# First batch of a fused attention and gated MLP: both heads' scores on half the rows each, and a shift of the weights' narrowing moved to GpSimd

## The chip, the cores and the metric

The kernel runs on one core of a Trainium2 chip. The metric is the device time of one execution in microseconds (us). PE is TensorE, DVE VectorE, ACT ScalarE, POOL GpSimd, SP SyncE, which here issues nearly all DMAs.

## The reference, cut

```python
# q, k, v: (4, 8, 768, 64) float32; w_in, conv_w, w_out: float64
scores = q @ k.T / sqrt(64)                      # keep: key < 4, or 0 <= row - key < 128
a = softmax(where(keep, scores, -1e9))
x = (a @ v) as (4, 768, 512)
h = relu(x @ w_in)                               # d_ff 1024
conv = sum(conv_w[k] * h shifted by k - 1 rows)  # 3 taps
out = (h * sigmoid(conv)) @ w_out
```

## The kernel before, in words

The function `banded` does the work. It takes the heads in pairs, 4 pairs to a batch, and the rows in tiles of 128, 6 to a pair; one tile of one pair is a step. The first batch has 24 steps (first rows 0 to 383 of all pairs, then the others), and it is computed in plain float32, while later batches use split operands.

A step goes through `scores` (a product for each of the two heads into a PSUM tile `sc` of its own, two buffers; a masked minimum over each on DVE, L577; an exponential each on ACT, L580; sums and reciprocals on DVE, L583 and L584; a normalisation each on POOL, L586), `transp` (transposes of the weights, L603, copied out by ACT, L605) and `pv` (products with the values, L655 and L678).

Before a half of a pair comes to its scores, `prep32` transposes three tiles of the queries of both heads at once (head 0 on partitions 0 to 63, head 1 on 64 to 127), and ACT copies them out twice (L288 through `evac`): plane `j` is multiplied by column `j` of `headscale`, which is zero on the other head's partitions. So the score product of one head reads all 128 partitions of queries and keys (L378), half of them zeros.

During the same 24 steps the float64 weights are loaded and narrowed, 17 pieces, one a step from step 2 on: 16 of 128x512, and the three taps as 24x128. `narrow` computes on the two 32-bit words of a value: ACT multiplies the high words, read as floats, by 2^-112 into `low` (L118); DVE shifts that left by 3 into `w` (L121); DVE ors in the low words shifted right by 29 (L122); DVE ors in the sign bit of `low` (L123). `split` then rounds `w` on POOL (L130) and takes the remainder on DVE (L131). `w` and `low` take buffers from a set of three.

From step 12 on the MLP's products of the first 256 rows (L204 up, L239 down, the gate between them L211 to L227) are interleaved with the steps; in the later batches they fill TensorE. A planner puts each engine's instructions in one order ahead of time from its own costs; at run time every engine goes through its own in that order. `follow` adds a wait of one instruction on another.

Of the kernel before, what the change touches and what calls it, by code (L numbers as in the profile page):

```python
# [10 lines left out]
F32 = mybir.dt.float32  # L11
F32R = mybir.dt.float32r
I32 = mybir.dt.int32
AF = mybir.ActivationFunctionType
ALU = mybir.AluOpType
PSUM = bass.MemoryType.PSUM

P = 128
D = 64
# [5 lines left out]
SW = 2 * P + NS  # L25
# [13 lines left out]
def f(ap):  # L39
    return ap.bitcast(F32)  # L40
# [6 lines left out]
def follow(c, ins, other, reason):  # L47
    c.tc.add_manual_dep(ins.ins, other.ins.name, mybir.DependencyInfo(mybir.DependencyClass.Sync, mybir.DependencyReason.DATA),
                        reason=reason)
# [17 lines left out]
class Moe:  # L67
# [41 lines left out]
    def narrow(self, raw, to=None):  # L109


        if raw.dtype == F32:
            return raw
        nc, (rows, n) = self.c.nc, raw.shape[0:2]
        w = self.temp("st", 512, 3)[0:rows, 0:n] if to is None else to
        low = self.temp("st", 512, 3)[0:rows, 0:n]
        lo, hi, wi, li = raw[:, :, 0], raw[:, :, 1], w.bitcast(I32), low.bitcast(I32)
        first = nc.scalar.mul(low, f(hi), 2.0 ** -112)  # L118
        if len(getattr(self.c, "exps", [])) > 1:
            follow(self.c, first, self.c.exps[-2], "late")  # L120
        nc.vector.tensor_scalar(wi, li, 3, None, ALU.logical_shift_left)  # L121
        nc.vector.scalar_tensor_tensor(out=wi, in0=lo, scalar=29, in1=wi, op0=ALU.logical_shift_right, op1=ALU.bitwise_or)  # L122
        nc.vector.scalar_tensor_tensor(out=wi, in0=li, scalar=-0x80000000, in1=wi, op0=ALU.bitwise_and, op1=ALU.bitwise_or)  # L123
        return w

    def split(self, raw, parts, at):
# [147 lines left out]
class Attn:  # L274
# [74 lines left out]
    def prep32(self, g, half, s, kk, tag, ahead):  # L349

        c, nc, T, HTL, kw = self.c, self.nc, self.T, self.HTL, self.kw
        tiles = slice(HTL * half, HTL * half + HTL)

        def turn(nm):
            pt = self.mps.tile([P, HTL, P], F32, tag=tag, name=f"tr{nm}{g}{half}", bufs=3 if tag == "h" else 2)
            for t in range(HTL):
                c.pin(nc.tensor.transpose(pt[:, t, :], s.raw[nm, half][:, t].rearrange("p a d -> p (a d)"), c.ident))
            if nm == "q":
                s.X[half] = f(self.ap.tile([P, 2, HTL, P], F32R, tag="X", name=f"X{g}{half}", bufs=3))
                for j in range(2):  # L360
                    self.evac(s.X[half][:, j], pt, c.headscale[:, j:j + 1])
            else:
                s.kk = kk
                self.evac(kk[:, tiles, 0:P], pt, 1.0)
                if half == 0:
                    nc.scalar.copy(kk[:, :, P:kw], kk[:, 0:1, 0:kw - P].to_broadcast([P, T, kw - P]))
            ahead()

        s.plain = True
        return [lambda nm=nm: turn(nm) for nm in "qk"]  # L370

    def scores(self, s, t, pcs, lo, hi):

        half, u = divmod(t, self.HTL)
        X, kk = s.X[half], s.kk.rearrange("p a t k -> p a (t k)") if not s.plain else s.kk.rearrange("p t k -> p (t k)")
        if s.plain:
            for j, pc in enumerate(pcs):
                self.c.pin(self.nc.tensor.matmul(pc, X[:, j, u, :], kk[:, lo:hi], start=True, stop=True))  # L378
            return
        for j, pc in enumerate(pcs):  # L380
            self.c.pin(self.nc.tensor.matmul(pc, X[:, j, u, :], kk[:, j, lo:hi], start=True, stop=False))  # L381
            self.c.pin(self.nc.tensor.matmul(pc, X[:, j, u, :], kk[:, 2 + j, lo:hi], start=False, stop=True))  # L382
# [68 lines left out]
def banded(c):  # L451

    nc = c.nc
# [48 lines left out]
        nc.gpsimd.memset(sm, 1e-9)  # L502
    A.tiles = 0
    c.exps = []
    c.zero = nc.gpsimd.to_reg(0.0)
    c.part = cp.tile([P, 2], F32, name="part")
    nc.gpsimd.memset(c.part, 1.0)
# [43 lines left out]
    def scores(g, t):  # L551
        s = st[g]
        apart = g < NPAIR
        at = P if apart else 0
        lo = 0 if t == 0 else (t - 1) * KW
        mk = m0 if t == 0 else ((w1, w2) if apart else (m1, m2))[t > 1]
        cols = slice(at + NS if t == 0 else 0, at + KW)
        sm = sms[A.tiles % len(sms)]
        A.tiles += 1
        hf, u = divmod(t, 3)  # L560
        if u == 0:
            if apart:
                s.pe[hf] = m.room[g % 2][:, 0:6 * SW].rearrange("p (t h k) -> p t h k", t=3, h=2)
            else:
                s.pe[hf] = ap.tile([P, 3, 2, KW], F32, tag="pe", name=f"pe{g}_{hf}")
            if t == 0:
                nc.gpsimd.memset(s.pe[hf][:, 0, :, at:at + NS], 0.0)
        pe = s.pe[hf][:, u]
        pcs = [ps.tile([P, SW], F32, tag="sc", name=f"sc{g}_{t}_{j}", bufs=2) for j in range(2)]
        if t == 0:  # L570
            A.scores(s, t, [pc[:, KW:SW] for pc in pcs], lo, lo + P)
        else:
            A.scores(s, t, pcs, lo, lo + SW)
        for j, pc in enumerate(pcs):
            if t and not apart:
                nc.vector.copy_predicated(pc[:, KW:SW], before.bitcast(I32), pc[:, 0:P])
            nc.vector.tensor_tensor_reduce(out=pe[:, j, cols], in0=pc[:, P - at:SW][:, cols], in1=mk, op0=ALU.add, op1=ALU.min,  # L577
                                           scale=1.0, scalar=3.0e38, accum_out=sm[:, j:j + 1])
        for j in range(2):
            exp = nc.scalar.activation(pe[:, j, cols], pe[:, j, cols], AF.Exp, bias=sm[:, j:j + 1], scale=-1.0,  # L580
                                       accum_out=sm[:, 2 + 2 * j:3 + 2 * j])
        c.exps.append(exp)
        nc.vector.tensor_reduce(out=sm[:, 6:8], in_=sm[:, 2:6].rearrange("p (j e) -> p j e", e=2), op=ALU.add, axis=mybir.AxisListType.X)  # L583
        nc.vector.reciprocal(sm[:, 8:10], sm[:, 6:8])  # L584
        for j in range(2):
            nc.gpsimd.tensor_scalar(pe[:, j, cols], pe[:, j, cols], sm[:, 8 + j:9 + j], 1.0, ALU.mult, ALU.mult)  # L586
# [147 lines left out]
    for i in range(NST + DL):  # L734
        if i < NST:
            n, g, t = steps[i]
            if t % 3 == 0:
                for n1, at, *ends in coming(n):
                    new = prep(n1)
                    if at is None:  # L740
                        at = [ends[0] + (ends[1] - ends[0]) * (k + 1) / len(new) for k in range(len(new))]
# [16 lines left out]
        for slot in range(SLOTS):  # L758
            if slot == 0 and i < NST:
                first(i, scores, g, t)  # L760
            if slot == 0 and 0 <= i - D2 < NST:
                first(i, transp_sinks, *steps[i - D2][1:])
            if slot == (1 if i - D1 < NSTB else 2) and 0 <= i - D1 < NST:
                first(i, transp, *steps[i - D1][1:])
            for d, at in ((D2, 2), (DL, 1)):
                if slot == at and 0 <= i - d < NST and (i - d < NSTB) == (d == D2):
                    first(i, pv, *steps[i - d][1:])
                    if i - d + 1 in cuts:
                        while fill:
                            fill.pop(0)()  # L770
                        lo, hi, span = cuts[i - d + 1]
                        fill = m.pieces(lo, hi)
                        rate = len(fill) / (span - 0.5)
                        acc = 0.0
            acc += rate / SLOTS
            while acc >= 1.0 and fill:
                fill.pop(0)()
                acc -= 1.0
            while todo and i + (slot + 1) / SLOTS >= todo[0][0]:
                first(i, todo.pop(0)[1])  # L780
# [75 lines left out]
def attention_gated_mlp(ctx: ExitStack, tc: tile.TileContext, q, k, v, n_sink, window, w_in, conv_w, w_out, out):  # L856
    nc = tc.nc
    c = Ctx()
# [4 lines left out]
    con = ctx.enter_context(tc.tile_pool(name="con", bufs=1))  # L863
# [13 lines left out]
    nc.scalar.activation(fl[:, 0:1], fl[:, 1:2], AF.Exp)  # L877
    c.ident = con.tile([P, P], F32, name="ident")
    make_identity(nc, c.ident)
    c.headscale = con.tile([P, 2], F32, name="headscale")  # L880
    nc.gpsimd.memset(c.headscale, 0.0)
    for j in range(2):
        nc.gpsimd.memset(c.headscale[D * j:D * j + D, j:j + 1], -1.0 / math.sqrt(D))
    c.identr = con.tile([P, P], F32R, name="identr")
    nc.vector.tensor_copy(c.identr, c.ident)

# [19 lines left out]
    with tc.If(fast == 1) as cmp:  # L906
        with ExitStack() as es:
            c.es = es
            banded(c)
# [32 lines left out]
```

## Time and profile before

| | us |
|---|---|
| median of 3 runs | 474.14 (473.42 to 474.23) |
| the profiled execution, whole | 473.48 |
| its span, first to last instruction | 471.8 |
| mean granted TensorE clock | 0.997 of full speed |

Times in rows are from the span's start. The whole time has 1.7 us around the span. A row's busy time is what the profile shows for an instruction, blocked time within it included; two instructions of one engine can overlap a little in it.

### The profile page before, as it was taken

Reading aid. Unit: us, or ns where it says so; the run is one execution under the profiler, and the core shown is the slowest. Engines: PE = TensorE matmul, PEld = TensorE weight load, DVE = VectorE, ACT = ScalarE, POOL = GpSimd, SP = SyncE. Lnnn points to the kernel's source line nnn. Section 1 sums busy time; section 2 is a strip of 40 time slices with the busy share of each in tenths; the row PEclk is TensorE's granted clock in tenths of the full one; section 3 lists DMA queues with packets and bytes.
Section 4 is the critical chain, followed back from the end, with each engine's and each line's share of the span. In section 5 each row is a group of like instructions: output and inputs, shape, how many; then the busy total and the mean of one; then the engine's idle time right before and its main releaser. Section 6 shows DMA issues by size and latency. Waiting matters only on the chain.

```text
span 471.8 us, 10560 instructions
## 1 busy us (share of the span) xinstructions
PE 444.6 (94%) x3181; PEld 388.3 (82%) x3181; DVE 339.0 (72%) x1190; ACT 321.3 (68%) x1027; POOL 281.3 (60%) x557
## 2 busy tenths in 40 slices
PE   3898989898899999999999999999999999999994
PEld 3576768697798988898989898988989898998982
DVE  4799999758858668786766859685767663665562
ACT  4989957768867868785867767675857654554542
POOL 3474786626858658676755757667656671445340
PEclk9999999999999999999999999999999999999998
DMA  6888674388667472655273655545250101000001
GB/s 140 219 229 251 183 201 107 81 199 203 167 153 179 137 175 68 161 146 133 61 192 81 166 119 134 143 120 124 71 141 15 46 1 46 0 23 24 24 24 53
DMA packets 105851, 55.91 MB, mean 119 GB/s; under 512 B 83072, under 2 KB 98712, under 8 KB 105784
## 3 DMA queue, kind: packets, MB, share of 16 engines
q1 hardware_dynamic: 105640, 55.00, 45.5%
q8 instruction: 28, 0.46, 0.4%
q14 instruction: 39, 0.32, 0.2%
q10 hardware_dynamic: 144, 0.13, 0.1%
HBM read 28.17 MB, written 6.29 MB: 73 GB/s over the span
## 4 chain that ended last, share of the span: by engine, by line
PE 75%; DVE 11%; ACT 4%; POOL 3%; DMA 2%; issue 2%; DVEq 0%; POOLq 0%; ACTq 0%
PE ph L204 26%; PE po L239 25%; PE px L655 7%; PE sc L382 3%; PE sc L381 3%; PE pts L617 3%; PE px L678 2%; DVE stm L122 2%; PE tq L305 1%; PE tk L331 1%; DVE stm L123 1%; DMA kk<-bk 1%; DMA raw<-in_q_dram 1%; DVE roomH L577 1%; DVE roomL L577 1%
## 5 line engine op out<-in xcount | busy, mean ns | idle before, releaser
L239 PE MATMUL po<-woH,g 128*128 128x512 f32 x384 | 138.2, 405 | 1.5 <-POOL g L226 0.8
L204 PE MATMUL ph<-xH,wiH 128*128 128x258 f32 (+1 forms) x384 | 110.7, 288 | 0.0
L204 PE MATMUL ph<-xL,wiH 128*128 128x258 f32 (+1 forms) x384 | 109.6, 286 | 0.0
L204 PE MATMUL ph<-xH,wiL 128*128 128x258 f32 (+1 forms) x384 | 109.1, 284 | 0.0
L226 POOL TENSOR_SCALAR g<-t 128x256 fp32r<-128x256 f32 x94 | 44.3, 472 | 74.5 <-DVE t L219 50.6
L586 POOL TENSOR_SCALAR pe<-pe,sm 128x132 f32<-128x132 f32 (+1 forms) x144 | 62.8, 447 | 37.7 <-DVE sm L584 19.2
L239 PEld LDWEIGHTS po<-woH,g 128*128 128x128 f32 x384 | 69.4, 189 | 13.2 <-POOL g L226 1.7
L227 POOL TENSOR_TENSOR g<-t,g 128x256 fp32r<-128x256 f32 x94 | 74.5, 793 | 5.8
L239 PE MATMUL po<-woL,g 128*128 128x512 f32 x192 | 76.1, 396 | 0.0
L216 DVE SCALAR_TENSOR_TENSOR t<-hb,cw,t 128x256 f32<-128x256 f32 x96 | 53.8, 560 | 29.4 <-ACT t L215 28.9
L204 PEld LDWEIGHTS ph<-xH,wiL 128*128 128x128 f32 x384 | 72.8, 190 | 2.2
L204 PEld LDWEIGHTS ph<-xH,wiH 128*128 128x128 f32 x384 | 72.7, 189 | 2.0
L204 PEld LDWEIGHTS ph<-xL,wiH 128*128 128x128 f32 x384 | 72.7, 189 | 1.6
L580 ACT ACTIVATE pe<-pe,sm 128x132 f32<-128x132 f32 (+1 forms) x144 | 58.2, 406 | 14.4 <-DVE sm L577 12.8
L218 ACT ACTIVATE t<-t 128x256 f32<-128x256 f32 x96 | 40.1, 418 | 36.3 <-DVE t L217 35.9
L219 DVE SCALAR_TENSOR_TENSOR t<-t,hb 128x256 f32<-128x256 f32 x96 | 48.3, 504 | 15.1 <-ACT t L218 14.3
L215 ACT ACTIVATE t<-hb,cw 128x256 f32<-128x256 f32 x96 | 49.0, 511 | 12.4 <-POOL g L227 10.1
L217 DVE SCALAR_TENSOR_TENSOR t<-hb,cw,t 128x256 f32<-128x256 f32 x96 | 54.4, 567 | 4.0 <-POOL pe L586 0.5
L211 ACT ACTIVATE hb<-ph 128x258 f32<-128x258 f32 (+1 forms) x96 | 36.8, 384 | 17.4 <-PE ph L204 13.9
L577 DVE CUSTOM_DVE_ANT_0 pe<-sc,m 128x132 f32<-128x132 f32 (+1 forms) x144 | 39.8, 287 | 7.7 <-PE sc L382 6.9
L381 PE MATMUL sc<-kk,X 128*128 128x260 f32 (+1 forms) x144 | 42.3, 304 | 1.5 <-issue 1.1
L655 PE MATMUL px<-pT,vraw 128*64 128x128 f32 (+1 forms) x512 | 43.0, 317 | 0.0
(161 smaller groups left out, 896.1 us busy)
## 6 DMA issues: line engine op xcount, KB each, us to landing
X<-bq SPq DMA_DIRECT2D x96, 96.0 KB
vraw<-in_v_dram SPq DMA_DIRECT2D x16, 384.0 KB
out_dram<-stm SPq DMA_DIRECT2D x23, 256.0 KB
kk<-kk SPq DMA_DIRECT2D x24, 198.0 KB
raw<-in_k_dram SPq DMA_DIRECT2D x24, 192.0 KB
raw<-in_q_dram SPq DMA_DIRECT2D x24, 192.0 KB
kk<-bk SPq DMA_DIRECT2D x48, 96.0 KB
raw<-in_q_dram SPq DMA_DIRECT2D x16, 96.0 KB
```

The costliest lines, as they stand in the source:

```text
L204: self.latest = nc.tensor.matmul(u.h[:, 0:W], w[:, cc, ff * P:(ff + 1) * P], x[:, cc, t0:t1], start=(i == 0), stop=(i == len(prods) - 1))
L215: nc.scalar.mul(a, prev, cw[:, 0, ff:ff + 1])
L216: nc.vector.scalar_tensor_tensor(out=e, in0=this, scalar=cw[:, 1, ff:ff + 1], in1=a, op0=ALU.mult, op1=ALU.add)
L217: nc.vector.scalar_tensor_tensor(out=a, in0=nxt, scalar=cw[:, 2, ff:ff + 1], in1=e, op0=ALU.mult, op1=ALU.add)
L219: nc.vector.scalar_tensor_tensor(out=a, in0=e, scalar=1.0, in1=this, op0=ALU.add, op1=ALU.mult)
L227: nc.gpsimd.tensor_tensor(out=u.g[:, 1], in0=a, in1=f(u.g[:, 0]), op=ALU.subtract)
L239: ins = nc.tensor.matmul(po[:, 0:c.DM], u.g[:, a, tt * P:(tt + 1) * P], w[:, ff, :], start=(ff == 0 and i == 0), stop=(ff == NFF - 1 and i ...
L381: self.c.pin(self.nc.tensor.matmul(pc, X[:, j, u, :], kk[:, j, lo:hi], start=True, stop=False))
L577: nc.vector.tensor_tensor_reduce(out=pe[:, j, cols], in0=pc[:, P - at:SW][:, cols], in1=mk, op0=ALU.add, op1=ALU.min, scale=1.0, scalar=3. ...
L580: exp = nc.scalar.activation(pe[:, j, cols], pe[:, j, cols], AF.Exp, bias=sm[:, j:j + 1], scale=-1.0, accum_out=sm[:, 2 + 2 * j:3 + 2 * j])
L586: nc.gpsimd.tensor_scalar(pe[:, j, cols], pe[:, j, cols], sm[:, 8 + j:9 + j], 1.0, ALU.mult, ALU.mult)
L655: ins = nc.tensor.matmul(px[h][D * j:D * j + D, P * at:P * at + n], s.v[:, j, kt, :], pT, start=(h not in open_), stop=False, skip_group_c ...
```

## The change

Queries are copied out once, both heads in one plane, with the scale as a constant; `headscale` and its memsets go. The score product of head `j` takes partitions 64j to 64j+63 of queries and keys alone. The first of the two products of a step also waits for the last masked minimum issued before it (that of head 1 in the step before). In `narrow` POOL writes `low * 0 * 1` (a zero with the sign of `low`) into `w`; DVE then ors in the low words as before, and its last instruction ors in `low` shifted left by 3, which drops the sign bit that `w` already has. DVE has two instructions a piece in the place of three, POOL two in the place of one.

```diff
@@ narrow
-        nc.vector.tensor_scalar(wi, li, 3, None, ALU.logical_shift_left)
+        nc.gpsimd.tensor_scalar(w, low, 0.0, 1.0, ALU.mult, ALU.mult)
         nc.vector.scalar_tensor_tensor(out=wi, in0=lo, scalar=29, in1=wi, op0=ALU.logical_shift_right, op1=ALU.bitwise_or)
-        nc.vector.scalar_tensor_tensor(out=wi, in0=li, scalar=-0x80000000, in1=wi, op0=ALU.bitwise_and, op1=ALU.bitwise_or)
+        nc.vector.scalar_tensor_tensor(out=wi, in0=li, scalar=3, in1=wi, op0=ALU.logical_shift_left, op1=ALU.bitwise_or)
@@ prep32
-                s.X[half] = f(self.ap.tile([P, 2, HTL, P], F32R, tag="X", name=f"X{g}{half}", bufs=3))
-                for j in range(2):
-                    self.evac(s.X[half][:, j], pt, c.headscale[:, j:j + 1])
+                s.X[half] = f(self.ap.tile([P, 2, HTL, P], F32R, tag="X", name=f"X{g}{half}", bufs=3))[:, 0]
+                self.evac(s.X[half], pt, -1.0 / math.sqrt(D))
@@ Attn.scores
-                self.c.pin(self.nc.tensor.matmul(pc, X[:, j, u, :], kk[:, lo:hi], start=True, stop=True))
+                r = slice(D * j, D * j + D)
+                ins = self.c.pin(self.nc.tensor.matmul(pc, X[r, u, :], kk[r, lo:hi], start=True, stop=True))
+                if self.c.reduced is not None and j == 0:
+                    follow(self.c, ins, self.c.reduced, "both together")
@@ scores in banded: c.reduced is the latest masked minimum
-            nc.vector.tensor_tensor_reduce(out=pe[:, j, cols], in0=pc[:, P - at:SW][:, cols], in1=mk, op0=ALU.add, op1=ALU.min,
-                                           scale=1.0, scalar=3.0e38, accum_out=sm[:, j:j + 1])
+            c.reduced = nc.vector.tensor_tensor_reduce(out=pe[:, j, cols], in0=pc[:, P - at:SW][:, cols], in1=mk, op0=ALU.add,
+                                                       op1=ALU.min, scale=1.0, scalar=3.0e38, accum_out=sm[:, j:j + 1])
@@ attention_gated_mlp
-    c.headscale = con.tile([P, 2], F32, name="headscale")
-    nc.gpsimd.memset(c.headscale, 0.0)
-    for j in range(2):
-        nc.gpsimd.memset(c.headscale[D * j:D * j + D, j:j + 1], -1.0 / math.sqrt(D))
```

## Rows read from the trace of the kernel before

**Rows 1.** Windows, us of each engine in five stretches, all instructions.
```profile
core 0: us, PE busy (x) PEld busy (x) DVE busy (x) ACT busy (x) POOL busy (x), PEclk, DMA share, GB/s
13.00:22.00 9.00, 7.57 (x42) 5.75 (x42) 7.52 (x32) 8.53 (x28) 4.16 (x7) 1.00 0.70 186
22.00:55.00 33.00, 28.39 (x223) 22.61 (x222) 31.31 (x105) 29.08 (x92) 21.54 (x34) 1.00 0.86 239
55.00:90.00 35.00, 31.20 (x220) 25.37 (x219) 33.88 (x89) 24.95 (x73) 24.40 (x32) 1.00 0.46 123
90.00:200.00 110.00, 106.66 (x824) 93.99 (x823) 79.63 (x345) 84.11 (x296) 71.64 (x154) 1.00 0.66 161
200.00:472.00 272.00, 265.23 (x1864) 236.23 (x1862) 180.99 (x593) 169.00 (x529) 155.19 (x303) 0.99 0.32 82
```

**Rows 2.** Chain of waits by line, shares of 22 to 90 us, then of 13 to 22.
```profile
by line: DVE stm L122 12.4%; DVE stm L123 9.2%; issue 8.2%; DVE roomH L577 6.3%; DVE roomL L577 6.0%; DVE woL L131 5.5%; DVE stm L121 4.6%; DVE xL L390 4.1%; PE sc L378 3.9%; DVE wiL L131 3.9%; POOL roomL L586 3.3%; DVE t L217 2.8%; DVE t L
...
by line: DMA raw<-in_q_dram 54.0%; ACT roomL L580 24.1%; ACT X L288 22.1%; ACT roomH L580 16.5%; PE trq L357 9.7%; ACT pT L605 9.4%; ACT kks L288 6.6%; ACT stm L118 6.4%; DMA kks<-in_v_dram 5.2%; ACT kks L366 1.1%; issue 1.1%
```

**Rows 3.** Windows of L121 alone, DVE us and count.
```profile
22.00:55.00 33.00, 4.83 (x9) 1.00 0.86 239
55.00:90.00 35.00, 3.85 (x6) 1.00 0.46 123
```

**Rows 4.** The tile of the narrowing, ns of one: shortest, median, longest.
```profile
L121 DVE TENSOR_SCALAR stm<-stm x16: 405/540/886, 13.7 to 80.4; 128x512 int32<-128x512 int32 x16
L123 DVE SCALAR_TENSOR_TENSOR stm<-stm,stm x16: 664/680/1193, 16.8 to 84.3; 128x512 int32<-128x512 int32 x16
L130 POOL TENSOR_SCALAR wiH<-stm x8: 612/618/787, 17.6 to 68.1; 128x512 fp32r<-128x512 f32 x8
```

**Rows 5.** Timeline, all engines: a POOL instruction of the new one's shape, and DVE beside it.
```profile
27.57 0.62 POOL L130 TENSOR_SCALAR wiH<-stm 128x512 fp32r<-128x512 f32 x1 [1.35 <-DVE sm L584]
27.59 0.88 DVE L121 TENSOR_SCALAR stm<-stm 128x512 int32<-128x512 int32 x1
...
28.39 0.41 DVE L577 CUSTOM_DVE_ANT_0 roomH<-sc,roomH 128x260 f32<-128x260 f32 x1
...
57.98 0.62 POOL L130 TENSOR_SCALAR wiH<-stm 128x512 fp32r<-128x512 f32 x1 [0.65 <-DVE sm L584]
58.00 0.89 DVE L121 TENSOR_SCALAR stm<-stm 128x512 int32<-128x512 int32 x1
...
80.14 0.78 POOL L130 TENSOR_SCALAR woH<-stm 128x512 fp32r<-128x512 f32 x1
...
80.36 0.84 DVE L121 TENSOR_SCALAR stm<-stm 128x512 int32<-128x512 int32 x1
...
85.46 0.41 DVE L577 CUSTOM_DVE_ANT_0 roomL<-sc,roomH 128x260 f32<-128x260 f32 x1
85.56 0.62 POOL L130 TENSOR_SCALAR woH<-stm 128x512 fp32r<-128x512 f32 x1 [0.64 <-DVE sm L583]
```

**Rows 6.** The normalisation L586 over 0 to 95 us, ns: shortest, median, longest.
```profile
L586 POOL TENSOR_SCALAR roomH<-roomH,sm x24: 375/723/1407, 14.0 to 87.5; 128x260 f32<-128x260 f32 x20, 128x128 f32<-128x128 f32 x4
```

**Rows 7.** Waits in 20 to 90 us: who waited for whom, total, times, longest.
```profile
POOL woH L130 <- DVE stm L123: 6.5, 4, 2.4
POOL g L226 <- DVE t L219: 6.4, 4, 2.8
PEld pts L603 <- POOL roomH L586: 3.4, 5, 0.9
DVE wiL L131 <- POOL wiH L130: 0.4, 1, 0.4
DVE roomH L577 <- PE sc L378: 0.3, 1, 0.3
```

**Rows 8.** ACT's copies L288 over 0 to 95 us, ns as above.
```profile
L288 ACT ACTIVATE X<-trq,headscale x16: 562/578/602, 7.9 to 73.2; 128x384 f32<-128x384 f32 x16
L288 ACT ACTIVATE kks<-trk x8: 469/482/512, 8.8 to 76.3; 128x384 f32<-128x384 f32 x8
```

**Rows 9.** Chain of waits in order: start, us, engine, tile, line, count.
```profile
90.67 0.44 PE sc L378 x2
...
91.54 0.33 PE pts L603 x3
...
93.27 1.46 PE px L655 x24
94.73 0.87 PE px L678 x6
...
106.18 3.21 DMA kk<-bk
```

More of the change, by code (lines that the diff above doesn't have):

```diff
@@ L504, in banded @@
     c.exps = []
+    c.reduced = None
     c.zero = nc.gpsimd.to_reg(0.0)
```

## The prediction

> **What bounds the kernel now.** I read the windows first, cut where the character of the work changes [rows 1]. From 200 us on PE is busy 265 of 272 us, from 90 to 200 us 107 of 110: there the kernel runs at PE's pace, and the change alters none of that work. So what the first 90 us gain or lose should reach the end nearly whole, and only they need a sum. Within them the windows name two stretches. From 22 to 90 us DVE is busy 31.3 + 33.9 = 65.2 of 68 us, PE 59.6, ACT 54.0, POOL 45.9 [rows 1]: DVE is the bound. From 13 to 22 us ACT is the busiest, 8.5 of 9 us.
>
> The chain of waits confirms it by line [rows 2]. In 22 to 90 us its largest parts are DVE's: the narrowing (L122, L123, L131, L121 add up to 12.4 + 9.2 + 9.4 + 4.6 = 36%) and the masked minima (12%). In 13 to 22 us it is ACT: exponentials and the copies of the queries. PE's scores are 3.9% of the long stretch. The reader is to see that the two edits meet different engines: the sign bits touch the bound, the scores an engine with slack.
>
> **The shift leaves DVE.** L121 runs 9 + 6 times in 22 to 90 us for 4.83 + 3.85 = 8.7 us [rows 3]. Neighbouring DVE records overlap by some 0.08 us (0.88 from 27.59 ends at 28.47, the next starts at 28.39 [rows 5]), so its place on DVE is 8.7 - 15 x 0.08 = 7.5 us. The two pieces before 22 us lie where ACT binds: nothing. L122 and L123 keep shape and operand count, so they keep their price.
>
> **The same bits come back on POOL.** The nearest row is L130: POOL, tensor_scalar, 128x512, one float32 input, 0.612 us at least, 0.618 in the middle [rows 4]; 15 x 0.62 = 9.3 us more on an engine busy 45.9 of 68. That alone would be covered, since POOL mostly waits for DVE (6.5 and 6.4 us for L123 and L219 [rows 7]).
>
> But the two engines do not run independently. At 27.57 a POOL L130 starts, at 27.59 a DVE L121, and that takes 0.88 us where its shortest is 0.405 [rows 4, 5]; the L130 is not longer than alone. The same pair at 57.98 gives 0.89, at 80.14 0.84. In the other direction L586, 0.375 us at its shortest, has a median of 0.72 in this stage [rows 6]: POOL is stretched too. The minimum L577, which reads one operand from PSUM, shows nothing: 0.41 beside the L130 at 85.56, as elsewhere [rows 5].
>
> This is the term that decides, so I went through all 15 L130 of 22 to 90 us in the timeline of both engines and took, for the DVE instruction that starts during one, its time less the shortest of its line. Eleven delay DVE (first 0.47 us at 27.57, last 0.43 at 80.14), the rest fall beside L577 or other PSUM readers and cost nothing; the sum is 3.8 us, 0.26 us each. The ends are 0 (as at 85.56) and 0.48 (as at 57.98), so 0 to 7.2 us for 15 new ones. I take the mean, 3.8 us, because the new instruction has L130's shape and stands in the same mix.
>
> [...]
>
> Of L121's own 8.7 us, 15 x 0.405 = 6.1 is work and 2.6 is such blocking. POOL's instructions that blocked it stay, and will meet the DVE instruction that moves up: if that is a two-operand one the wait moves, if it is L577 it is gone. Between 0 and 2.6 I take half, 1.3 us.
>
> **A new hop in each piece.** Before, L122 waited for DVE's own L121; now ACT's `low` goes to POOL and L122 waits for POOL. Behind a waiting L122 stand the minima of the steps, hence exponentials, transposes and `pv`; behind the POOL instruction stand L586, for which PE waited 3.4 us in its longest entry already [rows 7], and the rounding of the gate. The only like wait before is L131 on L130: once, 0.4 us, in 15 pieces [rows 7]. Ends: 0, and 15 x 0.4 = 6 us. I take 0.6: the planner has other DVE work to put between, as it did for L131. Covering this is POOL's slack of 22 us in 68; if POOL ran late everywhere, the 6 us would be due.
>
> **One copy of the queries less.** Eight halves lose one L288 of 0.58 us, and the other falls from 0.578 to about 0.482, the copy of the keys with a constant scale [rows 8]. From 28 us on ACT has slack: nothing. In 13 to 28 us two halves are copied, some 2 x 0.55 = 1.1 us; DVE is itself near full from 22 us, so between 0 and 1.1 I take 0.5. The first two halves come before 13 us, where a load of the queries holds the chain (the part of 54% in the row of 13 to 22 us is one load, which ends at its start [rows 2]): nothing. The memsets of `headscale` run while POOL waits at the start: nothing.
>
> **Scores on half the rows.** A head's product of 260 columns is two records, 0.44 us in sequence [rows 9], a step 0.88. No row shows two products on two halves of the rows. The nearest are L655, two heads on two halves of the columns: 24 records of 128 in 1.46 us, 0.061 each, where transposes of 128, on the whole array, take 0.33 / 3 = 0.11 [rows 9]. The heads there must overlap. If so here, the second record of head 0 runs with the first of head 1 and a step takes three units in the place of four, 0.66 us; fully overlapped 0.44. Against it stand the products L678 on 96 rows, 0.87 / 6 = 0.145 a record where a whole-array one takes 0.11 [rows 9]: 0.035 us dearer, which on 96 score records would be 3.4 us of PE. The 18 steps after 22 us so give PE between 18 x 0.44 = 7.9 us back, and at the other end cost some 2.5 us. PE is not the bound there; on the chain scores are 3.9% of 68, 2.65 us [rows 2]. So on the path it is -1.3 (halved) to +0.4 (0.035 on 0.22); I take the three units, a quarter of 2.65: -0.7.
>
> [...]
>
> The added wait makes head 0 wait for a minimum of 0.41 us more [rows 5]. Queued behind it are the products of the MLP and transposes. DVE waited for scores once, 0.3 us [rows 7], since it has other work between two steps; and PE has a slack of 8 us. I take nothing, and 18 x 0.41 us of PE's slack if the cover goes.
>
> **Sum.** -7.5 (L121) + 3.8 (new blocking) + 1.3 (blocking moved) + 0.6 (hop) - 0.5 (ACT) - 0.7 (scores) = -3.0 us. The profiled execution, 473.5, would become 470.5; the median of the runs stands 0.65 above it, so the forecast for a median is 474.1 - 3.0 = 471.1. All ends together give -7.5 - 1.1 - 1.3 = -9.9 and -7.5 + 7.2 + 2.6 + 6.0 + 0.4 = +8.7.
>
> **Rivals.**
> - *The two engines shut each other out* (slower). Place: L122 and L123 against POOL. Price: 15 x 0.48 = 7.2 and the 2.6 stays whole: -7.5 + 7.2 + 2.6 + 0.6 - 1.2 = +1.7, 475.8 us. With the moved blocking at 1.3 it decides from a mean delay of (7.5 - 1.3 - 0.6 + 1.2) / 15 = 0.45 us per new instruction on. For it: in 22 to 90 us DVE's 65.2 and POOL's 45.9 busy us hold much waiting already. Against: the measured mean is 0.26. [...] 21%.
> - *The hop takes it back* (no change). POOL is late in 55 to 90 us, where the gate's work comes on top (24.4 of 35 us, plus 7 x 0.62 = 28.7, in less time); L122 waits 0.25 us a piece, 3.7 in the place of 0.6: 474.2 us. Against: only one wait for L130 before. 14%.
> - *DVE keeps nearly all of it* (faster than forecast). The new instructions fall beside the minima, blocking 1 us in all, none moved, no hop: -7.5 + 1.0 - 0.5 - 0.7 = -7.7, 466.4 us. For it: four of 15 L130 delay nothing. 17%.
> - *The scores don't overlap*: a record stays 0.22 us, and the edit gives only ACT's share: 471.8 us. 8%.
> - The forecast: 40%.
>
> **Range and chances.** For no rival is the end sharp; cutting some 1 in 10 at each side, 466 to 476 us holds 8 in 10. About 0.2% (0.9 us) is what a measurement of this kernel can tell from no change. Faster: forecast, scores that don't overlap, and DVE's full gain, 40 + 8 + 17 = 65%; same 14%; slower 21%.
>
> **What would show it.** L121 gone, 17 more POOL instructions of about 0.62 to 0.79 us. L123 with a median near its 0.68 [rows 4] supports the 0.26; near 1 the first rival. Waits of L122 for POOL: under 1 us in total, or the second. L288 on X eight times at 0.48. Score records: starts of a pair within 0.7 us. PE's first product after the last score of the batch (score records of 90.67 now [rows 9]) comes 3 us earlier. The prediction is wrong if DVE in 22 to 87 us has idle time of several us (then another engine set the pace), or if what is gained by 90 us is lost again before 200, where a move of the keys by DMA sits on the chain for 3.2 us [rows 9].

## The result: 1.5% slower

The changed kernel takes 481.48 us (median of 5 runs, 480.13 to 482.07) where the kernel before takes 474.14: a ratio of 1.0148, 95% interval 1.0119 to 1.0178. Forecast were 471.1 us, 466 to 476. Size and sign are wrong. In the code after, L577, L580, L583, L584, L586, L603, L655 and L678 have become L580, L583, L586, L587, L589, L606, L658 and L681; L121 is now POOL's instruction.

The windows of the changed kernel, for [rows 1]:

```profile
core 0: us, PE busy (x) PEld busy (x) DVE busy (x) ACT busy (x) POOL busy (x), PEclk, DMA share, GB/s
13.00:22.00 9.00, 7.45 (x28) 4.26 (x27) 5.68 (x24) 6.23 (x20) 5.14 (x9) 1.00 0.69 179
22.00:55.00 33.00, 29.17 (x200) 19.97 (x201) 25.20 (x87) 24.38 (x78) 22.52 (x37) 0.84 0.74 204
55.00:90.00 35.00, 30.58 (x222) 23.78 (x221) 31.89 (x81) 25.26 (x69) 29.37 (x39) 0.95 0.57 154
90.00:200.00 110.00, 105.68 (x808) 91.43 (x807) 83.87 (x337) 82.88 (x289) 72.25 (x150) 1.00 0.63 157
```

From 22 to 55 us DVE is busy 25.2 us where it was 31.3: it has the idle time that the prediction named as the sign that another engine sets the pace. PE's instructions in the first two stretches are 28 and 200 where they were 42 and 223, though PE is about as busy. And PEclk, 1.00 for both in [rows 1], is 0.84 and 0.95.

PE's counts are the best measure here, since both kernels have the same 3181 in all (an instruction across a window's edge is counted in both windows). Two windows of the kernel before, whose third, 200 to 472 us, is in [rows 1]; then three of the changed one:

```profile
13.00:100.00 87.00, 77.17 (x563) 62.58 (x562) 78.53 (x241) 70.00 (x211) 54.07 (x80) 1.00 0.68 181
100.00:200.00 100.00, 96.66 (x741) 85.13 (x741) 73.80 (x329) 76.67 (x275) 67.68 (x147) 1.00 0.64 158
```
```profile
13.00:100.00 87.00, 75.94 (x517) 54.73 (x516) 71.45 (x215) 63.42 (x192) 63.70 (x93) 0.92 0.63 170
100.00:200.00 100.00, 96.94 (x737) 84.71 (x737) 75.19 (x311) 75.33 (x264) 65.56 (x139) 1.00 0.65 162
200.00:478.00 278.00, 271.92 (x1914) 242.38 (x1912) 186.74 (x621) 175.76 (x553) 160.41 (x314) 1.00 0.31 83
```

By 100 us the changed kernel is 46 PE instructions behind, by 200 us 50; they are done after 200 us, where one takes 272 / 1864 = 0.146 us. 50 x 0.146 = 7.3 us, where the medians differ by 7.3 us and the spans of the two profiled executions by 6.5: that is the loss. The middle stretch hardly differs. So the question is why PE gets less done before 100 us.

PE's level there, from windows of the changed kernel, and its chain of waits by line in 13 to 22 us:

```profile
26.00:36.00 10.00, 7.72 (x74) 5.34 (x73) 8.69 (x29) 6.39 (x22) 8.89 (x14) 1.00 0.66 192
36.00:38.00 2.00, 1.24 (x7) 0.97 (x8) 1.92 (x10) 1.61 (x6) 0.00 (x0) 0.61 0.82 188
38.00:46.00 8.00, 7.87 (x41) 4.82 (x39) 5.98 (x24) 6.54 (x23) 5.37 (x9) 0.50 0.45 136
```
```profile
by line: DMA raw<-in_q_dram 54.3%; PE sc L378 43.4%; PE trq L357 18.9%; PE pt L606 11.6%; PE trk L357 7.2%; DVE stm L122 6.6%; DVE roomH L580 5.3%; DMA kks<-in_v_dram 4.7%; issue 4.3%; DVE sm L580 1.1%; DVE sm L586 0.8%; DVEq L580 0.1%
```

In 38 to 46 us the granted clock is 0.50. In 13 to 22 us the chain, behind the load that ends at its start, is now led by PE's scores and transposes, where ACT led it in [rows 2]. PEclk reads 1.00 there, but only because the kept trace has its first record of the level at 26.2 us (at 14.9 in the kernel before) and nothing counts as lost ahead of it; the durations tell the level. PE's timeline of the changed kernel, early and late (start, us of the group, count):

```profile
15.11 1.24 PE L378 MATMUL sc<-kks,X 64*128 64x260 f32 x4
...
18.72 0.90 PE L357 MATMUL trq<-ident,raw 128*128 128x128 f32 x3
...
50.00 0.49 PE L357 MATMUL trq<-ident,raw 128*128 128x128 f32 x3
50.42 0.71 PE L378 MATMUL sc<-kks,X 64*128 64x260 f32 x4
```

And of the kernel before:

```profile
15.44 0.49 PE L357 MATMUL trk<-ident,raw 128*128 128x128 f32 x3
```

A transposition of three tiles takes 0.90 at 18.7 and 0.49 at 50.0; a pair of scores (two products of two records each) 1.24 at 15.1 and 0.71 at 50.4. In the kernel before, three transposes take 0.49 from 15.44 on. At its lower level PE is not an engine with slack: from 18 to 26 us it is busy 8.0 of 8 us.

### The profile page after: what moved, and what is told of

Its sections match the earlier page's. It is cut to its first block, busy times and chain, and to the rows that moved or that the text cites. A ratio compares the mean times of both kernels' runs of the same rounds, so it can differ in the third digit from the quotient of the medians.

```text
span 478.3 us, 10549 instructions
## 1 busy us (share of the span) xinstructions
PE 450.8 (94%) x3181; PEld 385.5 (81%) x3181; DVE 338.8 (71%) x1173; ACT 319.2 (67%) x1019; POOL 293.7 (61%) x571
## 4 chain that ended last, share of the span: by engine, by line
PE 78%; DVE 6%; POOL 5%; issue 3%; ACT 3%; DMA 3%; SPq 0%; POOLq 0%; ACTq 0%; DVEq 0%
PE ph L204 26%; PE po L239 26%; PE px L658 7%; PE sc L383 3%; PE sc L384 3%; PE pts L620 3%; PE px L681 2%; PE sc L378 2%; POOL roomL L589 2%; DMA kk<-bk 2%; PE tk L331 1%; PE tq L305 1%; DVE stm L122 1%; DMA raw<-in_q_dram 1%; POOL roomH L589 1%
## 5 line engine op out<-in xcount | busy, mean ns | idle before, releaser
L589 POOL TENSOR_SCALAR pe<-pe,sm 128x132 f32<-128x132 f32 (+1 forms) x144 | 65.0, 463 | 37.4 <-DVE sm L587 28.7
L226 POOL TENSOR_SCALAR g<-t 128x256 fp32r<-128x256 f32 x94 | 42.9, 456 | 64.6 <-DVE t L219 42.0
L227 POOL TENSOR_TENSOR g<-t,g 128x256 fp32r<-128x256 f32 x94 | 72.4, 771 | 5.9
L583 ACT ACTIVATE pe<-pe,sm 128x132 f32<-128x132 f32 (+1 forms) x144 | 58.0, 404 | 19.4 <-DVE sm L580 18.7
L218 ACT ACTIVATE t<-t 128x256 f32<-128x256 f32 x96 | 40.1, 418 | 31.5 <-DVE t L217 31.3
L219 DVE SCALAR_TENSOR_TENSOR t<-t,hb 128x256 f32<-128x256 f32 x96 | 49.3, 513 | 16.5 <-ACT t L218 16.0
L579 DVE COPY_PREDICATED sc<-before,sc 128x128 f32<-128x128 int32 x120 | 33.4, 288 | 17.4 <-PE sc L384 16.8
L658 PE MATMUL px<-pT,vraw 128*64 128x128 f32 (+1 forms) x512 | 43.7, 322 | 1.3 <-ACT pT L608 1.3
```

Of the source, the lines that this page charges most:

```text
L219: nc.vector.scalar_tensor_tensor(out=a, in0=e, scalar=1.0, in1=this, op0=ALU.add, op1=ALU.mult)
L226: nc.gpsimd.tensor_scalar(u.g[:, 0], a, 1.0, 1.0, ALU.mult, ALU.mult)
L227: nc.gpsimd.tensor_tensor(out=u.g[:, 1], in0=a, in1=f(u.g[:, 0]), op=ALU.subtract)
L658: ins = nc.tensor.matmul(px[h][D * j:D * j + D, P * at:P * at + n], s.v[:, j, kt, :], pT, start=(h not in open_), stop=False, skip_group_c ...
```

## The experiments

Each is the kernel before with the edit named, timed beside the kernel before on the same chip. "PE" is the count and the busy us of its window 13 to 100 us, and that window's PEclk, from the one profiled execution; it is left empty where that execution is not like those compared (e3, h1) or the count holds other products (f1). That of h2 took 478.13 us, 2.9 above its median. "Rest" is the count of PE's instructions from 200 us to the end. A loss given in us below is the ratio less one, times the median of the kernel before.

| | ratio, 95% interval | us | PE: count, busy, clock | rest |
|---|---|---|---|---|
| before | | 474.0 to 475.0 | x563, 77.17, 1.00 | x1864 |
| e1 scores, with the wait | 1.0128 (1.0103 to 1.0153) | 480.62 | x540, 78.46, 0.94 | x1909 |
| e4 scores, no wait | 1.0102 (1.0075 to 1.0129) | 478.65 | x523, 82.87, 0.96 | x1901 |
| g1 half rows, two copies | 1.0134 (1.0098 to 1.0170) | 480.66 | x500, 81.62, 0.90 | x1911 |
| g2 one copy, all rows | 0.9989 (0.9967 to 1.0010) | 474.02 | x574, 78.12, 1.00 | x1850 |
| g3 half rows in the last 12 steps | 1.0097 (1.0059 to 1.0134) | 478.28 | x553, 78.73, 0.98 | x1878 |
| g4 half rows in the first 12 steps | 1.0153 (1.0112 to 1.0195) | 480.14 | x538, 81.12, 0.94 | x1901 |
| f1 e1 and one more product a step | 1.0255 (1.0217 to 1.0292) | 486.17 | | x1963 |
| e2 sign bits | 1.0115 (1.0089 to 1.0141) | 479.87 | x534, 76.27, 0.98 | x1912 |
| f2 L121 off DVE, nothing on POOL | 0.9997 (0.9973 to 1.0021) | 474.50 | x550, 77.24, 0.96 | x1874 |
| f3 the POOL instruction added | 1.0088 (1.0055 to 1.0121) | 478.49 | x532, 74.88, 0.96 | x1903 |
| h1 a DVE instruction added | 1.0083 (1.0055 to 1.0110) | 478.26 | | |
| h2 sign bits by ACT | 0.9993 (0.9973 to 1.0013) | 475.28 | x534, 77.36, 0.94 | x1900 |
| e3 the whole change, no wait | 1.0137 (1.0103 to 1.0171) | 480.71 | | |
| f4 another order | 1.0005 (0.9982 to 1.0029) | 474.80 | x575, 78.53, 1.00 | x1872 |

What a rest has beyond the 1864 of before, times 0.146 us, comes within 2 us of what the span of that execution lost. The counts by 100 us can tell less: e1 is only 23 instructions behind there, and 45 at 200.

The mean granted clock of every run was noted as well. Over the runs compared it is 0.996 for the kernel before in each set, 0.993 for f2, 0.990 for f3, 0.989 for g3 and 0.991 for h1 and h2. A difference of 0.001 is 0.47 us of PE's time at its upper level, so falls of the level took some 1.5 us more than before in f2, 2.9 in f3, 3.2 in g3 and 2.4 in h1 and h2. h2 loses nothing all the same, so such a sum is not yet a loss at the end.

### The two edits apart: e1 and e2

e1 has the diff without its three lines of `narrow`, e2 those three lines alone.

> The scores' part alone (one plane of queries, products on half the rows, the added wait); the narrowing as before. Theory 'clock': the half-row products leave TensorE at its lower level for long (in the changed kernel its records run at half pace up to 26 us and from 37 to 47 us), and this part alone costs most of the 7 us: 477 to 481 us, with low stretches before 50 us. Theory 'POOL': the second POOL instruction of a piece is what costs, and this part alone gives back a little: 472 to 474 us, whatever the clock shows.

> The sign bits on POOL alone; the scores as before. Theory 'clock': TensorE stays at its upper level after 15 us and the prediction's sum for the narrowing holds: 470 to 473 us. Theory 'POOL': L122 waits for POOL, POOL for DVE, and both block each other: 478 to 482 us at an undisturbed clock.

Either alone costs most of what both cost: 6.1 and 5.5 us (0.0128 and 0.0115 of 474.28), 7.0 together (0.0148 of 474.14). e1 came as "clock" had it and e2 as "POOL" had it, though "POOL" had the clock undisturbed and e2's is 0.98. Both edits are wrong in sign, and their losses overlap.

### The added wait: e3 and e4

e3 is the whole change without `follow(self.c, ins, self.c.reduced, "both together")`, e4 is e1 without it.

> The changed kernel without the added wait of the first score product of a step on the last masked minimum. Theory 'wait': the wait costs the 7 us: 473 to 476 us. Theories 'clock' and 'POOL': it hardly matters: 479 to 483 us.

> The scores' part alone without the added wait. Theory 'wait': 472 to 474 us, where the scores' part with the wait is slower by several us. Theory 'clock': the same as with the wait within 2 us. Theory 'POOL': 472 to 474 with or without it.

Without the wait the ratio is 0.0011 and 0.0026 lower, 0.5 and 1.2 us, with intervals that overlap: not resolved. Nor is the wait all that differs: it keeps the two products of a step side by side on PE. In the kept traces the second product's record starts with the first's (within 0.03 us) in 45 of 48 cases in e1 and 43 in the changed kernel, but in 20 in e4, 19 in g1, 14 of 24 in g3 and 5 of 24 in g4, which have no wait; what a product standing apart costs is in the step on the scores below. The rest of the scores' loss, 4.8 us in e4, has another cause than the wait.

### What of the scores costs: g1, g2, g3, g4

g1 has half rows and still the two copies with `headscale`:

```diff
+                r = slice(D * j, D * j + D)
-                self.c.pin(self.nc.tensor.matmul(pc, X[:, j, u, :], kk[:, lo:hi], start=True, stop=True))
+                self.c.pin(self.nc.tensor.matmul(pc, X[r, j, u, :], kk[r, lo:hi], start=True, stop=True))
```

g2 has the one copy of the change and `X[:, u, :]` with `kk[:, lo:hi]`, all rows, so that both heads get the sum of the two heads' scores. g3 (`whole = half == 0`) and g4 (`whole = half == 1`) have two copies and all rows in one half of the steps, one copy and half rows in the other:

```diff
+                r = slice(0, P) if whole else slice(D * j, D * j + D)
+                self.c.pin(self.nc.tensor.matmul(pc, X[r, j if whole else 0, u, :], kk[r, lo:hi], start=True, stop=True))
```

> Before, with score products on half rows alone: the queries are still copied twice with headscale, and no wait is added. Theory 'pace' (half-row products keep TensorE at its lower level until some 27 us and the early steps come at its pace): the loss is that of e4, 478 to 479.5 us, transposes of three at 0.8 us until after 20 us. Theory 'order' (the loss comes from the copy that ACT no longer makes, through another order of the work): 474 to 475 us, with transposes of three at 0.33 to 0.5 us by 16 us.

> Before, with one copy of the queries, both heads in one plane, and score products on all 128 rows: both heads then get the sum of the two heads' scores, so the computation is changed there; no wait is added. Theory 'pace': no loss, and the half microsecond of ACT that the prediction gave to the copy, 473 to 474.5 us. Theory 'order': the loss of e4, 478 to 479.5 us, though TensorE reaches its upper level by 16 us.

> The first 12 steps (rows 0 to 383) as before, with two copies and products on all rows; the last 12 with one copy and half rows; no wait is added. Theory 'pace': the level rises by 16 us as before, and 4.7 us of the loss by 33 us go: 474 to 475.5 us, a little more if the level falls again after 37 us. [...]

> The reverse: the first 12 steps with one copy and half rows, the last 12 as before; no wait is added. Theory 'pace': transposes of three at 0.8 us until after 20 us and the loss of e4 whole, 477.5 to 479 us. [...]

g1 and g2 part the edit cleanly: with half rows and all of ACT's copies the loss is there (6.4 us), with one copy and whole rows it is not. "Order" falls; g1 lies above the range of "pace", and so does g4. g4 shows the level at work, because its first 47 products and transposes are those of the kernel before, in the same order. Windows 13 to 33 and 33 to 100 us of the kernel before, then of g4:

```profile
13.00:33.00 20.00, 16.66 (x118) 13.04 (x118) 17.65 (x71) 17.91 (x61) 11.97 (x22) 1.00 0.83 228
33.00:100.00 67.00, 60.50 (x446) 49.54 (x444) 60.88 (x172) 52.09 (x151) 42.10 (x59) 1.00 0.63 167
```
```profile
13.00:33.00 20.00, 19.06 (x79) 11.66 (x79) 16.72 (x65) 14.63 (x49) 11.56 (x22) 0.74 0.74 200
33.00:100.00 67.00, 62.06 (x460) 49.48 (x461) 59.11 (x174) 52.02 (x152) 42.00 (x60) 1.00 0.62 166
```

In 20 us PE is busy longer, 19.06 for 16.66 us, and does 79 instructions for 118: it works, at a lower pace, and its half-row products, which mostly stand apart, are dearer too (at the upper level 0.63 us for 0.44, below). ACT, which led here, is busy 14.6 us in the place of 17.9. After 33 us, with whole rows again, PEclk is 1.00 and the counts are close to those of before. PE's timeline of g4, against 0.49 for the same three transposes at 15.44 before:

```profile
14.32 1.24 PE L381 MATMUL sc<-kks,X 64*128 64x260 f32 x4
15.49 0.90 PE L357 MATMUL trk<-ident,raw 128*128 128x128 f32 x3
```

Each kernel that began with half rows alone (the changed one, e1, e4, g1, g4) ran most of its transposes until some time between 24 and 34 us at 0.8 to 0.9 for three, with a short rise in g1 and g4 about 20 us (three take 0.65 at 19.51 us in g1, 0.55 at 19.36 in g4); each that began with whole rows (before, e2, f2, f3, f4, g2, g3, h2) reached 0.49 by 16 us. Why half rows hold the level is not shown; in g4 PE is busy 19.06 of the 20 us and the level is low all the same.

g3 is the miss. It is like the kernel before until 33 us (118 instructions, 16.65 us), and its level falls only late, yet it loses 4.6 us (2.8 to 6.4) where "pace" allowed 1.5. Windows of g3:

```profile
84.00:86.00 2.00, 0.34 (x2) 0.16 (x2) 2.00 (x6) 0.31 (x2) 1.93 (x2) 1.00 0.19 44
86.00:88.00 2.00, 2.00 (x13) 2.00 (x14) 1.61 (x5) 2.00 (x8) 0.64 (x1) 0.70 0.00 0
88.00:90.00 2.00, 2.00 (x9) 1.57 (x7) 0.86 (x3) 0.93 (x4) 1.92 (x4) 0.50 0.86 196
```

In 84 to 86 us PE waits for normalisations on POOL, 1.2 and 0.6 us, and afterwards the level is 0.50 for some 4 us; that is some 2 us. In the kernel before the same two waits take 0.5 and 0.3 us, with no fall after them. This execution, 476.99 us, is one of the two quickest of six and has the highest clock of them, 0.994. By the mean, 0.989, falls of the level took 3.2 us more than in the kernel before, of the 4.6 lost, so most of the miss goes with further falls in executions whose traces were not kept. Its half-row products stand together in 7 of 12 steps and apart in 5, which by the prices below comes out near nothing. The halves do not add up either (g3 and g4 lose 4.6 and 7.3, g1 6.4). So the early half is settled as to the level, and what brings about the late falls stays open.

### More of TensorE's work in e1: f1

One product on all rows into the first `sc`, ahead of the two that count, in each step; the wait is on it.

```diff
+            ins = self.c.pin(self.nc.tensor.matmul(pcs[0], X[:, u, :], kk[:, lo:hi], start=True, stop=True))
+            if self.c.reduced is not None:
+                follow(self.c, ins, self.c.reduced, "both together")
```

> The scores' part alone, and before each pair of half-row products one whole-array product of the same size into the first PSUM tile, which the real one overwrites: 24 more products, some 10 us of TensorE at its upper level. Theory 'clock': the whole-array work holds TensorE at its upper level from about 15 us on, and in spite of the extra work the time falls from 480.6 to between 475 and 478 us. Theory 'order' (any change makes the planner set up another order, and the order of before is a good one): no better than 480 us. Theory 'wait': also no better than 480.

Three transposes take 0.52 already at 17.81 us, so the early pace is back. But "clock" forecast 475 to 478 us and is wrong here: 24 products of 0.44 us at PE's upper level are 10.6 us of work, the level falls to 0.50 in 40 to 46 and 54 to 60 us all the same (a pair takes 1.24 at 40.34 and 55.06, 0.71 at 51.21), and the loss is 12.1 us. That is less than e1's 6.1 and 10.6 together, but more than e1's. Bought like this, the level costs more than it gives.

### What L121 was worth: f2 and h1

f2 leaves the signs of the weights out, and so needs two instructions:

```diff
-        nc.vector.tensor_scalar(wi, li, 3, None, ALU.logical_shift_left)
...
+        nc.vector.tensor_scalar(wi, lo, 29, None, ALU.logical_shift_right)
+        nc.vector.scalar_tensor_tensor(out=wi, in0=li, scalar=3, in1=wi, op0=ALU.logical_shift_left, op1=ALU.bitwise_or)
```

h1 keeps the three of before and adds one, into the tile that POOL's rounding writes next:

```diff
+            nc.vector.tensor_scalar(extra, low, 1.0, 1.0, ALU.mult, ALU.mult)
```

> The kernel before, with the narrowing in two DVE instructions (low words shifted right by 29; then the float part shifted left by 3 or-ed in) and no POOL instruction: the sign bits are left out. It shows what DVE's shift is worth without its price on POOL. Theory 'POOL' (the second POOL instruction costs): 466 to 470 us, 7 us or nearly off the bound. Theory 'order': 474 to 480 us.

> Before, with one more DVE instruction of 128x512 with one input for each of the 16 pieces (low times 1 times 1 into the high part of the rounded weight, which POOL's rounding then overwrites); nothing else waits for it, and it falls 15 times between 22 and 90 us. Theory 'DVE is at its limit, and others are just behind it' (taking 7.5 us off it gave nothing because the chain of PE, ACT and POOL takes as long, adding must still cost): 15 times 0.41 to 0.54 is 6 to 8 us, 479 to 482 us. Theory 'DVE had slack though it was 96% busy' (its busy time was partly early work that nobody waits for): under 2 us, 474 to 476 us.

f2 is the edit as the prediction costed its first term, with nothing added anywhere: no gain, 474.5 us, and "POOL" with its 466 to 470 us is wrong. The window 13 to 100 us of f2, and what DVE waits for in 13 to 97 us:

```profile
13.00:100.00 87.00, 77.24 (x550) 63.59 (x549) 67.14 (x223) 67.43 (x207) 50.46 (x80) 0.96 0.65 178
```
```profile
DVE woL L130 <- POOL woH L129: 2.6, 3, 0.9
DVE xL L389 <- ACT xH L388: 2.3, 1, 2.3
DVE roomH L576 <- PE sc L377: 2.3, 5, 0.8
DVE stm L121 <- DMA wo0r<-in_moe_w_out_dram: 2.0, 1, 2.0
```

DVE works 67.1 us in the place of 78.5, and the 11 us freed are idle time: it waits for POOL, for ACT, for PE, for the DMA of the weights. PE is busy 77.24 us as before, 77.17, with 13 instructions fewer at a clock of 0.96. So DVE was busy 96% of 22 to 90 us and still not what set PE's pace; that it ran ahead where it could, behind engines that hardly had more to give, is the likeliest reading. By the mean clocks a gain of some 1.5 us may be hidden behind falls of the level, but not one of 7.5. Adding as much to DVE costs 3.9 us (2.6 to 5.2) for 15 x 0.41 to 0.54 = 6 to 8 us: between the two theories, and not the mirror of f2. DVE was at the edge, with several others.

### What POOL's instruction costs: f3 and h2

f3 leaves `narrow` as it was and adds `nc.gpsimd.tensor_scalar(extra, low, 0.0, 1.0, ALU.mult, ALU.mult)`, for which no DVE instruction of `narrow` waits. h2 is e2 with `nc.scalar.mul(w, low, 0.0)` in the place of POOL's instruction (the weights come out without their signs, as in f2).

> The kernel before, with one more POOL instruction a weight piece, 128x512, that reads low and writes where L130 writes later: nothing of DVE waits for it. It shows the price of the new POOL instruction without the new hop. Theory 'POOL, by blocking and queueing': 477 to 482 us. Theory 'hop' (L122 waiting for POOL is the price): 474 to 476 us. By the prediction's 0.26 us of blocking each it would be 474.1 + 3.8 = 478.

> Before, with the sign bits made by ACT in the place of POOL (low times zero into the weight, ACT 128x512) and DVE's two instructions of the changed kernel; scores as before. Theory 'POOL's instruction is the price' (DVE's gain is nothing, the POOL instruction costs 4 us and the hop 1.4): without it the loss goes but nothing is won, 473.5 to 475.5 us. Theory 'any third engine in the chain of a piece costs': ACT's 15 times 0.6 us and its order behind the exponentials make it late, 477 to 480 us, like e2. Theory of the prediction (DVE is the bound and ACT has 14 us of slack): 468 to 471 us.

f3: 4.2 us (2.6 to 5.7) for the instruction alone. PE's waits in f3, 13 to 97 us:

```profile
PE sc L380 <- DVE sm L579: 4.3, 4, 2.5
PE pts L605 <- POOL roomH L588: 4.0, 5, 1.3
PE pts L605 <- POOL roomL L588: 1.9, 3, 0.8
PE pt L605 <- POOL roomL L588: 1.1, 1, 1.1
```

And in the kernel before:

```profile
PE pts L603 <- POOL roomL L586: 1.8, 3, 0.8
PE pts L603 <- POOL roomH L586: 1.4, 3, 0.6
PE pt L603 <- POOL roomL L586: 0.9, 1, 0.9
```

The three lines with POOL add up to 7.0 us; before they were 4.1 (the line with DVE was 3.0). POOL's normalisations come later, behind the new instructions. DVE's third narrowing instruction has a median of 0.758 in f3 where it was 0.680 [rows 4], so the blocking is there too. And the level falls for some 3.4 us at 23.5 and again at 88.3 (the four score records of a step take 2.06 us from 23.40 and 1.83 from 87.53, 1.04 from 33.41), there after PE waited 2.5 us for DVE; by the mean clocks such falls took 2.9 us more than in the kernel before. h2, with a hop to ACT and without POOL, loses nothing: the price is POOL's, not a hop's as such. Leaving POOL out wins nothing either, as f2 said.

### The planner's order: f4

The kernel before with AHEAD = 150 in the place of 200: the same work in another order.

> The kernel before with nothing changed but the planner's priority offset of the attention's steps, 150 in the place of 200: the same instructions in another order on each engine. Theory 'order': 476 to 481 us. Theories 'clock' and 'POOL': 473 to 476 us.

No difference that can be measured, so a changed order alone need not cost anything. It is one order.

## Why the prediction was wrong, step by step

**"DVE is the bound", and -7.5 us for L121: failed, and it is the largest error.** f2 measures 0 (-1.3 to +1.0), with at most some 1.5 us hidden behind the level. The views cited [rows 1, 2] showed a busy engine and the largest shares of a chain; neither shows how far the next chain is behind. The prediction named this sign, idle time of DVE, but gave it no chance of its own.

**"That alone would be covered, since POOL mostly waits for DVE": failed.** POOL had 22 us of slack in 68, yet the instruction cost 4.2 us, seen as normalisations late for PE. It is luck that 4.2 is near the 3.8 us of the term for new blocking: the term was put on DVE, where the four lines of the narrowing take only 2.4 us more in f3 (48.6 us in 13 to 100 us where it was 46.2), and f2 shows that a microsecond less on DVE is not worth one. How much of f3's 4.2 is blocking, how much POOL's own lateness and how much the falls of PE's level was not separated. The 0.375 us read as L586's shortest [rows 6] is that of its 128x128 form; the shortest of 128x260 is 0.476, so POOL was stretched less than read.

**Blocking moved, 1.3, and the hop, 0.6: the sizes roughly right, the place wrong.** L122 and L123 hardly moved (medians of 128x512: 0.682 for L122, 0.688 before; 0.685 for L123, 0.680 before), L131 did. Tile of the narrowing in the changed kernel, ns of one, shortest, median, longest:

```profile
L121 POOL TENSOR_SCALAR stm<-stm x16: 611/620/896, 14.7 to 88.7; 128x512 f32<-128x512 f32 x16
L123 DVE SCALAR_TENSOR_TENSOR stm<-stm,stm x16: 670/685/1210, 17.9 to 92.1; 128x512 int32<-128x512 int32 x16
L131 DVE TENSOR_TENSOR woL<-stm,woH x8: 687/1057/1098, 43.6 to 93.7; 128x512 fp32r<-128x512 f32 x8
```

L131's medians rose from some 0.68 to 0.97 and 1.06; the three lines take 40.0 us in 13 to 100 us where they took 36.4, so 3.6 us of the 3.8 + 1.3 booked as blocking are seen. L122 waited for POOL once, for 0.4 us; L131 waited for L130 3.7 us in 13 to 97 us where it was 0.4 [rows 7]: the late arrival is one instruction further on than the prediction put it. e2 less f2 and f3 leaves 5.5 + 0.1 - 4.2 = 1.4 us for the hop, uncertain by more than itself.

**One copy less, -0.5.** g2: -0.5 us (-1.6 to +0.5). Right as far as it can be told.

**Scores on half the rows, -0.7: the length of a pair right by luck, PE's level left out.** At PE's upper level a pair takes 0.64 us, from 50.42 to the next product at 51.06, where 0.66 was expected and 0.88 was before. But it is not three units of 0.22 in the place of four. The first records of that pair in the changed kernel, then the second:

```profile
50.42 0.49 PE L378 MATMUL sc<-kks,X 64*128 64x260 f32 x2
```
```profile
50.75 0.39 PE L378 MATMUL sc<-kks,X 64*128 64x260 f32 x2
51.06 0.33 PE L658 MATMUL px<-pT,vraw 128*64 128x128 f32 x2
```

One head's product by itself, with what comes next, in e4, then in the kernel before:

```profile
37.79 0.70 PE L378 MATMUL sc<-kks,X 64*128 64x260 f32 x2
38.42 0.71 PE L679 MATMUL px<-sT,kks 96*128 96x128 f32 x4
```
```profile
42.67 0.60 PE L378 MATMUL sc<-kks,X 128*128 128x260 f32 x2
43.11 0.49 PE L603 MATMUL pts<-ident,roomL 128*128 128x128 f32 x3
```

In the kept trace the two heads' first records start 7 ns apart, and their second ones too: the products run side by side in whole. But a record takes 0.32 us in the place of 0.22, and two of 0.32 happen to last as long as three of 0.22. A half-row product that stands apart takes 0.63 where a whole-row one takes 0.44; the prediction's bound, 0.035 dearer a record, was too low.

The sum also priced PE at the one level that [rows 1] show, and this is the step that failed. With half rows from the start PE stays at the lower level to 26 us or later, but for the short rise in g1 and g4. A pair takes 1.24 there and three transposes 0.90 in the place of 0.49: 4.8 to 6.4 us lost (e4, e1, g1; in e4 and g1 products standing apart are part of it, in e1 hardly). "The scores meet an engine with slack" failed with it: the slack was PE's at its upper level.

**The added wait at nothing.** The cover named, 8 us of PE's slack, is gone in 13 to 33 us. e1 and e4 differ by 1.2 us, not resolved; and that the wait keeps a step's two products together, 0.64 us where they take 2 x 0.63 apart, had no price in the sum.

**"What the first 90 us gain or lose should reach the end nearly whole": right.** 50 instructions times 0.146 us.

None of the rivals was what happened. They varied POOL against DVE or left the scores without effect; none moved PE's clock, and the slow side of the range, 476, had no room for the scores.

## What to carry to other kernels

That an engine is busy 96% of a stretch doesn't make its time worth anything (f2 freed 11 us of DVE for a gain of 0): leave the work out and time that first; and where several engines stand at the edge, moving work from one to another can pay the receiver's price (4.2 us for POOL's instruction in f3) and gain nothing from the giver. For a kernel that ends at TensorE's pace, count TensorE's instructions done in both kernels by a time from which both run at its pace (200 us here): the deficit times the later time of one is close to the loss. Before making products narrower in rows, look at when TensorE gets to its upper level (here by 16 us with whole rows, between 24 and 34 with half rows), what the products around them cost at the lower one (three transposes 0.90 us for 0.49), and whether the two halves will stand side by side (a pair takes 0.64 us then, 2 x 0.63 apart).

## What was not expected of the hardware

- In 13 to 33 us TensorE's granted clock was 0.74 in g4 and 1.00 before, though at first it was issued the same products in the same order but for the rows of the scores. The level also falls once or twice later, to 0.50 (38 to 46 us in the changed kernel; in f2, which has whole rows, within 22 to 30 and 40 to 50 us, where PEclk is 0.79 and 0.83 on average and three transposes take 0.90 at 42.85 us), so half rows are not the only cause of a fall.
- PEclk can read 1.00 where the records run at the lower pace (13 to 26 us of the changed kernel, ahead of its first record of the level): the durations of a fixed operation are the better witness.
- A DVE instruction of 24x128, 0.275 us in the kernel before, took 1.62 beside three POOL instructions. It ends 0.13 us after the last of the three. Tile `hb` of the kernel before, then the timeline of the changed one:

```profile
L122 DVE SCALAR_TENSOR_TENSOR hb<-tapsr,hb x1: 275/275/275, 32.7 to 32.7; 24x128 int32<-24x128 int32 x1
```
```profile
34.34 0.61 POOL L130 TENSOR_SCALAR wiH<-stm 128x512 fp32r<-128x512 f32 x1
...
34.39 1.62 DVE L122 SCALAR_TENSOR_TENSOR hb<-tapsr,hb 24x128 int32<-24x128 int32 x1 [0.38 <-POOL hb L121]
...
34.94 0.94 POOL L589 TENSOR_SCALAR roomH<-roomH,sm 128x260 f32<-128x260 f32 x2
```
